# Softmax sums in an attention, SoLU and softplus kernel: reciprocals transposed as four columns and repeated by DMAs, and a planner that reckons loads at 240 GB/s

## The chip, the cores and the metric

The kernel runs on one core of one Trainium2 chip. The metric is device time in microseconds (us). A core has TensorE (PE, with its weight loads shown as PEld), VectorE (DVE), ScalarE (ACT), GpSimd (POOL) and SyncE (SP); each runs its own instructions in order and waits on semaphores for the others. Here SP issues nearly all DMAs.

## The reference

Three stages, all in float32, 2304 rows of 512 between them:

```python
scores = scale * np.matmul(q, k.transpose(0, 1, 3, 2))      # 4 batches, 8 heads, 576 rows, 64 wide
thresh = np.max(scores, axis=-1, keepdims=True) - tau
scores = np.where(scores >= thresh, scores, -1000000000.0)
scores = scores - np.max(scores, axis=-1, keepdims=True)
attn = np.exp(scores)
attn = attn / (np.sum(attn, axis=-1, keepdims=True) + 1e-09)
x = np.matmul(attn, v)                                       # -> x of 2304 x 512
h = x @ w_in                                                 # 512 -> 1024
e = np.exp(h - np.max(h, axis=-1, keepdims=True))
solu = h * (e / (np.sum(e, axis=-1, keepdims=True) + 1e-09))
ln = (solu - mu) / np.sqrt(var + 1e-06) * g_ln               # over the row
x = ln @ w_out                                               # 1024 -> 512
h = x @ w2_in                                                # 512 -> 2048
out = (np.maximum(h, 0) + np.log1p(np.exp(-np.abs(h)))) @ w2_out
```

## The kernel before

**Attention.** Two heads of a batch are a pair, with buffers q, k and v of which four pairs fit. An item is one pair with one or two tiles of 128 query rows (36 items: 8 of one tile, 28 of two); 8 more items take the last 64 rows of four heads. Of a tile, PE makes the scores (L393), DVE their row maximum (L349), ACT the exponential (L350), DVE the threshold and the row sum (L352). PE transposes the weights E (L368), ACT copies them out of PSUM (L371), and PE multiplies them with v (L429), which gives the item's x transposed: 64 rows of one head above 64 of the other, a query to a column. The rows are not divided before that, so each column must be multiplied by the reciprocal of its query's sum.

**The reciprocals, item(), L377 to L434.** The sums of an item are a [128, 2 or 4] tile, a query to a partition. DVE adds 1e-9 and takes the reciprocal (inverse(), L355 to L358). To turn them into rows, ACT spreads each column to 64 columns (rb, L402), PE transposes rb, one full 128x128 transpose for each tile (L408, 64 in all), and ACT copies the result to x in SBUF (L410, two buffers). DVE then multiplies the product in PSUM with x (ml, L432). Until that is done, the product's bank is held; there are four such banks (`w`) for transposes, products, the two later stages' partial sums and fillers.

**The later stages.** The weights of the first two-layer network (w_in, w_out) are loaded as 64-bit words, put together and split into a high and a low part by ACT and DVE (convert(); for four of them PE does the subtraction, L512 and L513). m1_unit() then runs nine units of 256 rows: matmuls (L567), SoLU and normalization, transposes (L610), matmuls (L627, L628), and a store of the result to DRAM (x2s). The second network reads it back (x2m) and runs 16 chunks of its inner width for five blocks of rows (L678, softplus on ACT and DVE, L701). Its output weights (raw_out) have room only once the first network is done.

**The order.** Nothing of the order is written by hand. plan_of() makes a list of operations, each with its engine, two costs in ns (how long it holds the engine, and when its result is there), what it follows, which buffers it takes and uses, and a due time. Plan.order() (L107) then lays them out like a simulation: at each step it takes, of the operations that could start, the one due first; on PE a change of the kind of matmul (R scores, Q scores of the last rows, C product with v, T transposes, G full-width products) adds a price from a table, weighed by STICK (L169). AHEAD says how much later than the earliest one an operation may start and still be chosen. Loads follow one another in one file: 0.5 us after the issue a load moves its bytes at 350 GB/s, and 1.9 us later it has landed (L192, L193). The model also follows PE's clock, and fills early idle time of PE with idle products (filler, L288). The kernel then issues every instruction in the order of the start times found. Due times are the tile's number plus a number from lists (JT, JA, JIT for items; LO and LAGS for units; LD, PREP, PLOAD, W2IN, W2OUT for loads).

Of the kernel before, what the change touches and what calls it, by code (L numbers as in the profile page):

```python
# [9 lines left out]
F32 = mybir.dt.float32  # L10
# [12 lines left out]
P = 128  # L23
# [4 lines left out]
JT = [0.34, 7.73, 0.9, -3.39, 0.54, 0.49, 0.42, 9.02, 0.11, 3.15, -3.13, -0.51, -5.45, 1.01, 1.21, 6.91, -4.6, 8.15, -0.49, -0.88, -1.72, -3.81, 4.75, 9.79, 2.6, 9.72, 9.11, -5.74, -0.21, 2.17, 6.22, 2.62, -2.76, -1.92, 0.89, -0.0, -0.65, 0.66, -0.91, -2.44, -7.92, -1.24, -0.04, -1.57]  # L28
JA = [5.05, -2.61, -3.21, 7.47, 3.78, 3.3, 5.1, 12.84, -4.94, 8.51, 17.33, -7.99, 2.58, -3.17, 5.64, -2.85, 16.01, 16.98, -1.89, 6.77, -1.19, 4.83, 12.32, 18.27, -6.3, 0.39, 12.91, 14.21, 3.05, -5.54, -0.8, -1.5, 4.55, -1.49, -10.83, 10.72, -1.44, -1.37, -9.39, -0.79, 3.84, 3.5, 3.33, 5.39]
LO = [-20.52, -32.27, -28.3, -62.18, -3.33, 1.52, -98.95, 31.75, -24.96]  # L30
# [9 lines left out]
LD = [-11.06, 0.35, 9.2, 14.07, 7.04, 12.77, 7.9, 34.61, 19.66, 38.52, 7.77, 68.68, 10.48, 84.79, 20.67, 17.31, 4.65, 8.82, 1.55, -62.61, -15.71, -19.93, 81.02, 16.74, 91.83, 70.72, 19.84, -5.66, -48.3, 4.79, -22.69, -44.85]  # L40
JIT = [-11.99, -8.79, -5.19, -5.48, 1.8, -10.03, 0.87, -8.03, 6.15, -0.57, 3.09, -24.47, 0.08, 2.59, -34.82, 4.62, 7.64, 16.92, 9.09, 3.38, -14.37, -6.4, -10.15, 3.76, -6.77, -11.43, -14.53, -18.35, -5.02, -26.2, -15.19, -13.01, -2.79, 0.51, -17.2, 8.63, -5.03, -12.19, -11.44, -4.71, -8.08, -1.06, -14.31, -9.49]
# [38 lines left out]
WARM = 130e3  # L80

# [7 lines left out]
class Plan:  # L89
# [17 lines left out]
    def order(self):  # L107
# [12 lines left out]
        mode, dma, done = "", 0, []  # L120
        win, work, slow = 0, {}, False
# [31 lines left out]
        while any(cand.values()):  # L153
# [62 lines left out]
def tile_attention_solu_softplus(ctx: ExitStack, tc: tile.TileContext, q, k, v, tau, w_in, w_out, g_ln, w2_in, w2_out, out):  # L216
# [22 lines left out]
    done = plan_of(nc, ctx, sb, const, ident, minus, pools, stacks, w1t, x2s, q, k, v, tau, w_in, w_out, g_ln, w2_in, w2_out, out).order()  # L239
# [24 lines left out]
def plan_of(nc, ctx, sb, const, ident, minus, pools, stacks, w1t, x2s, q, k, v, tau, w_in, w_out, g_ln, w2_in, w2_out, out):  # L264
# [5 lines left out]
    plan = Plan(dict(w=W_, s=S_, h2=4, E=NE, T=2, eT=NET, x=2, xr=NXR, xrT=1, q=NPAIR, k=NPAIR, v=NPAIR, ln=3, u=2,  # L270
# [22 lines left out]
    def load(eng, out, in_, kb, after=(), takes=(), uses=(), due=0.0):  # L293
        e = sp if eng == "SP" else act
        return op(eng, 620, None, lambda: e.dma_start(out=out(), in_=in_()), after=after, takes=takes, uses=uses, due=due, kb=kb)
# [3 lines left out]
    o_minus = op("ACT", 200, 300, lambda: act.activation(out=minus, in_=ident, func=AF.Copy, scale=-1.0), after=[o_ident], due=-60)  # L299
    o_table = op("ACT", 1300, 1300, lambda: act.preload_act_table_set("natural_log_exp_and_others"), due=-49.5)  # L300

    def queue(what, i):
        return "ACT" if f"{what}{i}" in ON_ACT else "SP"

    def load_qk(p, due):
# [4 lines left out]
        z["kq"], ql = [], []  # L310
# [3 lines left out]
        for h in range(2):  # L314
            r = slice(64 * h, 64 * h + 64)
            ql.append(load(queue("q", p), lambda r=r: q_.t[r, :], lambda h=h: q[p][:, 640 * h:640 * h + 576], 144, takes=() if h else [q_], uses=[q_] if h else (), due=due))
        z["scaled"] = op("ACT", 574, 678, lambda: act.activation(out=q_.t, in_=q_.t, func=AF.Copy, scale=0.125), after=ql, uses=[q_], due=due + 0.5)
# [37 lines left out]
    def inverse(n, w, sums, masks, due):  # L355
        rv = buf("at", "rinv", f"rinv{n}", [P, 4], bufs=4)
        o1 = op("DVE", 80, 170, lambda: dve.tensor_scalar_add(rv.t[:, 0:w], sums.t[:, 0:w], 1e-9), after=masks, takes=[rv], uses=[sums], due=due)
        return rv, op("DVE", 95, 180, lambda: dve.reciprocal(rv.t[:, 0:w], rv.t[:, 0:w]), after=[o1], uses=[rv], due=due)  # L358
# [18 lines left out]
    def item(n):  # L377
# [4 lines left out]
        sums = buf("at", "sums", f"sums{n}", [P, 4], bufs=4)  # L382
        E = [buf("at", "E", f"E{n}_{i}", [P, 1152], bufs=NE) for i in range(nt)]
        masks = {}
        for kk, i in enumerate(ts):
# [8 lines left out]
            sc = op("PE", 970, 1128, emit_s, after=z["kq"] + [z["scaled"]], takes=s, uses=[z["q"], z["k"]], due=j + JIT[n], mode="R")  # L394
# [6 lines left out]
        rb = buf("at", "rb", f"rb{n}", [P, 4, 64])  # L401
# [459 lines left out]
```

## Time and profile before

| | |
|---|---|
| median of 3 runs | 911.25 us (910.9 to 912.68) |
| the profiled execution | 914.37 us, of which its span is 912.6 us |
| PE busy | 899.6 us |
| DVE busy | 690.4 us |
| ACT busy | 591.1 us |
| moved by DMA | 64.63 MB |

The span runs from the first to the last instruction; the time is measured around it. A busy share counts the time in which an instruction is on an engine. Matmuls are pipelined, so a matmul's duration is longer than the distance to the next one's start; the cost of one in a run is read from the starts. A group of lines names what is written, an arrow, and what is read.

### The profile page before, as it was taken

To read this page: it belongs to the slowest core of one execution; us is meant where nothing else is said; L and a number is where in the kernel's file an instruction comes from. 1 tells how busy PE (TensorE), PEld (TensorE's weight loads), DVE (VectorE), ACT (ScalarE), POOL (GpSimd) and SP (SyncE) were. 2 spreads that over 40 slices of the span, in tenths; PEclk is the share of its full clock that TensorE was granted. 3 is DMA by queue.
4 is the path that set the end of the run, shared out by engine and by line. 5 is a ranking of instruction groups with operands and counts; after the bars stand their busy time and mean duration, and the time that the engine had idled before them with its cause. 6 is when DMAs were issued, how large, how long until landed. Compare 5 with 4: busy or idle time off the path is not lost.

```text
span 912.6 us, 14433 instructions
## 1 busy us (share of the span) xinstructions
PE 899.6 (99%) x5458; PEld 709.6 (78%) x5458; DVE 690.4 (76%) x1474; ACT 591.1 (65%) x1159; POOL 0.7 (0%) x6
## 2 busy tenths in 40 slices
PE   8999999999999999999999999999999999999998
PEld 6576676677677677788888878888888888888897
DVE  5999898898777778599958969985556555655565
ACT  6978887997778687676757746764444444444454
POOL 0000000000000000000000000000000000000000
PEclk9999999999999999999999999999999999999999
DMA  9405110230231000164414223430021001100010
GB/s 281 161 1 175 54 30 1 84 83 24 66 109 62 2 1 12 59 219 162 139 59 162 93 98 110 135 119 24 1 92 47 1 1 47 47 0 1 1 47 24
DMA packets 32052, 64.63 MB, mean 71 GB/s; under 512 B 3440, under 2 KB 12912, under 8 KB 31984
## 3 DMA queue, kind: packets, MB, share of 16 engines
q1 hardware_dynamic: 31104, 61.62, 20.8%
q10 hardware_dynamic: 880, 2.10, 0.8%
q8 instruction: 43, 0.70, 0.3%
q14 instruction: 25, 0.20, 0.1%
HBM read 49.55 MB, written 14.16 MB: 70 GB/s over the span
## 4 chain that ended last, share of the span: by engine, by line
PE 83%; DVE 7%; ACT 4%; DMA 4%; issue 1%; SPq 1%; ACTq 0%; DVEq 0%
PE w L701 21%; PE h L678 20%; PE w L567 8%; PE w L368 7%; PE w L429 6%; PE s L393 6%; PE w L627 6%; PE w L628 3%; PE w L610 1%; PE w L472 1%; DMA raw<-in_w_in_dram 1%; DVE E L352 1%; DVE nm L349 1%; PE s L450 1%; DMA q<-in_q_dram 1%
## 5 line engine op out<-in xcount | busy, mean ns | idle before, releaser
L678 PE MATMUL h<-x2m,w2h 128*128 128x512 f32 (+1 forms) x640 | 181.6, 368 | 0.0
L678 PEld LDWEIGHTS h<-x2m,w2h 128*128 128x128 f32 x640 | 116.5, 188 | 21.0
L349 DVE TENSOR_REDUCE nm<-s 128x1 f32<-128x576 f32 x144 | 102.7, 752 | 21.7 <-PE s L393 19.1
L678 PE MATMUL h<-x2m,w2l 128*128 128x512 f32 (+1 forms) x320 | 117.7, 368 | 0.0
L701 PE MATMUL w<-wo2h,gh 128*128 128x512 f32 x288 | 112.9, 392 | 1.1 <-ACT wo2h L503 1.1
L701 PE MATMUL w<-wo2l,gh 128*128 128x512 f32 x288 | 113.0, 393 | 0.6 <-DVE wo2l L505 0.6
L352 DVE SCALAR_TENSOR_TENSOR E<-E,etau 128x576 f32<-128x576 f32 x128 | 101.1, 815 | 16.3 <-ACT E L350 14.9
L701 PE MATMUL w<-wo2h,gl 128*128 128x512 f32 x288 | 112.7, 391 | 0.0
L371 ACT COPY eT<-w 128x512 f32<-128x512 f32 (+1 forms) x188 | 92.9, 554 | 19.5 <-PE w L368 18.9
L689 ACT ACTIVATE t<-h 128x512 f32<-128x512 f32 (+1 forms) x80 | 44.3, 554 | 90.9 <-PE h L678 90.9
L627 PE MATMUL w<-lhl,wo1h 128*128 128x512 f32 x288 | 102.8, 397 | 0.0
L350 ACT ACTIVATE E<-s,nm 128x576 f32<-128x576 f32 x128 | 91.6, 756 | 11.2 <-DVE nm L349 11.0
L691 DVE TENSOR_SCALAR gw<-t 128x512 f32<-128x512 f32 (+1 forms) x80 | 31.8, 399 | 80.3 <-ACT t L690 80.1
L693 ACT ACTIVATE gw<-gw 128x512 f32<-128x512 f32 (+1 forms) x80 | 47.1, 589 | 61.1 <-DVE t L692 60.0
L393 PE MATMUL s<-k,q 64*128 64x288 f32 x512 | 83.9, 429 | 2.0 <-ACT E L350 1.4
L628 PE MATMUL w<-lhl,wo1l 128*128 128x256 f32 x288 | 80.7, 280 | 0.0
L429 PE MATMUL w<-eT,v 128*64 128x256 f32 (+1 forms) x720 | 77.8, 364 | 1.6 <-ACT eT L371 1.5
L368 PE MATMUL w<-ident,E 128*128 128x128 f32 x576 | 78.4, 279 | 0.0
L368 PEld LDWEIGHTS w<-ident,E 128*128 128x128 f32 x576 | 63.6, 141 | 17.4 <-issue 6.4
L694 DVE SCALAR_TENSOR_TENSOR gw<-h,gw 128x512 f32<-128x512 f32 (+1 forms) x80 | 51.0, 637 | 33.1 <-ACT gw L693 32.0
L429 PEld LDWEIGHTS w<-eT,v 128*64 128x64 f32 x720 | 47.1, 138 | 28.0 <-ACT eT L371 4.4
L678 PEld LDWEIGHTS h<-x2m,w2l 128*128 128x128 f32 x320 | 60.3, 188 | 10.1
(107 smaller groups left out, 1573.2 us busy)
## 6 DMA issues: line engine op xcount, KB each, us to landing
x2s<-x SPq DMA_DIRECT2D x36, 256.0 KB, 2.0
x2m<-x2s SPq DMA_DIRECT2D x18, 512.0 KB, 6.0
raw_in<-in_w_in_dram SPq DMA_DIRECT2D x16, 512.0 KB, 3.8
raw_out<-in_w_out_dram SPq DMA_DIRECT2D x16, 512.0 KB, 3.6
v<-in_v_dram SPq DMA_DIRECT2D x15, 320.0 KB, 3.4
q<-in_q_dram SPq DMA_DIRECT2D x28, 144.0 KB, 3.6
out_dram<-yo SPq DMA_DIRECT2D x15, 256.0 KB, 2.1
raw<-in_w_out_dram SPq DMA_DIRECT2D x3, 1024.0 KB, 7.8
```

The lines of the kernel that those rows point to most:

```text
L349: mx = op("DVE", 668, 750, lambda: dve.tensor_reduce(out=nm.t, in_=src(), axis=AX.XY, op=ALU.max, negate=True), after=[after], takes=[nm], ...
L350: ex = op("ACT", 638, 741, lambda: act.activation(out=dst().rearrange("p (a b) -> p a b", a=2), in_=src(), func=AF.Exp, bias=nm.t, scale=1.0),
L352: return op("DVE", 739, 900, lambda: dve.scalar_tensor_tensor(out=dst(), in0=dst(), scalar=etau, in1=dst(), op0=ALU.is_ge, op1=ALU.mult, a ...
L368: pe.transpose(bk.t[:, P * i:P * i + P], b_.t[:, c:c + P], ident)
L371: copies.append(op("ACT", occ, occ + 111, lambda: act.copy(out=eT.t[:, 0:width], in_=bk.t[:, 0:width]), after=[g], uses=[bk, eT], due=due))
L393: pe.matmul(s[h].t[:, nh, 0:288], z["q"].t[r, c:c + P], z["k"].t[r, 288 * nh:288 * nh + 288], start=True, stop=True)
L429: pe.matmul(o_.t[64 * h:64 * h + 64, 0:W], z["v"].t[:, vcols(c, h)], e[8 if c == 8 else 4 * h + c](), start=(i == 0), stop=(i == 4))
L567: pe.matmul(ps.t, x__[:, part, :], w_[:, part, 512 * n:512 * n + 512], start=(part == 0 and j_ == 0), stop=(part == 3 and j_ == 2))
L627: pe.matmul(o.t.rearrange("p (a q) -> p a q", a=2), w1t["wo1h"][:, c, P * m:P * m + P], lhl.t[:, :, c, :], start=(c == 0), stop=False)
L628: pe.matmul(o.t[:, 0:256], w1t["wo1l"][:, c, P * m:P * m + P], lhl.t[:, 0, c, :], start=False, stop=(c == 7))
L678: pe.matmul(ps.t[:, 0:n], w2t["in", a, c][:, part, :], x.t[:, b_, part, 0:n], start=(part == 0 and j_ == 0), stop=(part == 3 and j_ == 2))
L701: pe.matmul(ys[j].t, g_.t[:, P * j:P * j + P], w2t["out", a, c], start=(c == 0 and i == 0), stop=(c == NC2 - 1 and i == 2))
```

## The change

Four things. The reciprocals, a [128, w] tile with w of 2 or 4, are transposed as they are: one transpose an item gives [w, 128] in PSUM, ACT copies it to r4 (two buffers), SP writes it to a DRAM tile rs and reads it back with two DMAs, one for each head, which repeat each row to 64 partitions of x. q of the first pair is loaded and scaled in two pieces, columns 0 to 191 and 192 to 575, and the scores of its first tile wait for the first piece alone. The planner reckons loads at 240 GB/s rather than 350, the first not before 2.5 us, adds 1.8 us to the landing of the two reads, starts with PE's clock low, and has other costs for some operations. All lists of due times, STICK and AHEAD have other values.

```diff
-JT = [0.34, 7.73, 0.9, ...]
+JT = [1.36, -8.49, 3.75, ...]
...
-LAGS = [246.6, 85.18, 40.19, 34.26, 25.47, 27.39, 40.09, 53.12, 104.33]
-D_MAX, D_MASK, D_SUM, D_T, D_X, D_AV = 1.74, 10.86, 3.2, 3.73, 1.71, -15.06
-D_MT, D_POST, D_OUT = 8.93, 2.73, -15.88
-AHEAD = dict(PE=0, DVE=0, ACT=0, SP=20, POOL=20, X=20)
+LAGS = [303.47, 28.54, 2.25, 23.85, 74.05, 70.66, 42.32, 71.52, 102.15]
+D_MAX, D_MASK, D_SUM, D_T, D_X, D_AV = -7.0, 24.35, 5.23, 2.69, -23.16, 4.18
+D_MT, D_POST, D_OUT = 12.15, -13.18, -25.57
+AHEAD = dict(PE=20, DVE=100, ACT=20, SP=200, POOL=20, X=20)
...
-YLAG = 4.72
-PLOAD = -16.03
-W2IN = 60.61
-W2OUT = -5.81
+YLAG = 6.0
+PLOAD = -125.2
+W2IN = -10.08
+W2OUT = -10.85
 TURNED = 4
-STICK = 0.48
-PREP = [-18.8, -45.68, -12.55, 12.05, 71.4, 119.39, -150.07, 43.1]
+STICK = 1.85
+PREP = [-67.7, -87.23, -5.21, 2.75, 195.54, 111.21, -68.22, 79.77]
...
+FIRST = 2500
...
-        mode, dma, done = "", 0, []
-        win, work, slow = 0, {}, False
+        mode, dma, done = "", FIRST, []
+        win, work, slow = 0, {}, True
...
-                dma = max(dma, s + 500) + o.kb * 1024 / 350
-                o.end = dma + 1900
+                dma = max(dma, s + 500) + o.kb * 1024 / 240
+                o.end = dma + 1900 + (o.fin or 0)
...
+    rs = [dram.tile([4, P], F32, tag=f"rs{n}", name=f"rs{n}") for n in range(len(items_of()))]
...
-        z["scaled"] = op("ACT", 574, 678, lambda: act.activation(out=q_.t, in_=q_.t, func=AF.Copy, scale=0.125), after=ql, uses=[q_], due=due + 0.5)
+        cuts = [0, 192, S] if p == 0 else [0, S]
+        z["scaled"] = []
+        for a, e in zip(cuts, cuts[1:]):
+            ql = []
...
+            z["scaled"].append(op("ACT", occ, occ + 104, lambda a=a, e=e: act.activation(out=q_.t[:, a:e], in_=q_.t[:, a:e], func=AF.Copy, scale=0.125), after=ql, uses=[q_], due=due + 0.5))
...
-        rb = buf("at", "rb", f"rb{n}", [P, 4, 64])
-        o3 = op("ACT", 187 if nt == 1 else 310, 298 if nt == 1 else 410, lambda: act.copy(out=rb.t[:, 0:w, :], in_=rv.t[:, 0:w].unsqueeze(2).to_broadcast([P, w, 64])), after=[o2], takes=[rb], uses=[rv], due=jl + D_SUM)
         rbk = bank()
+        r4 = buf("at", "r4", f"r4{n}", [4, P], bufs=2)
         x = buf("at", "x", f"x{n}", [P, 256], bufs=2)
-
-        def emit_r():
-            for i in range(nt):
-                pe.transpose(rbk.t[:, P * i:P * i + P], rb.t[:, 2 * i:2 * i + 2, :].rearrange("p a b -> p (a b)"), ident)
-        rg = op("PE", 109 * nt, 109 * nt + 163, emit_r, after=[o3, o_ident], takes=[rbk, x], uses=[rb], due=jl + D_X, mode="T")
-        xc = op("ACT", 162 if nt == 1 else 263, 270 if nt == 1 else 395, lambda: act.copy(out=x.t[:, 0:W], in_=rbk.t[:, 0:W]), after=[rg], uses=[rbk, x], due=jl + D_X)
+        rg = op("PE", 64, 227, lambda: pe.transpose(rbk.t[0:w, 0:P], rv.t[:, 0:w], ident), after=[o2, o_ident], takes=[rbk], uses=[rv], due=jl + D_X, mode="T")
+        rc = op("ACT", 160, 265, lambda: act.copy(out=r4.t[0:w, :], in_=rbk.t[0:w, 0:P]), after=[rg], takes=[r4], uses=[rbk], due=jl + D_X)
+        wr = load("SP", lambda: rs[n][0:w], lambda: r4.t[0:w, :], 1, after=[rc], uses=[r4], due=jl + D_SUM)
+        xc = [load("SP", lambda h=h: x.t[64 * h:64 * h + 64, 0:W].rearrange("p (i q) -> p i q", q=P), lambda h=h: bass.AP(tensor=rs[n].tensor, offset=rs[n].offset + P * h, ap=[[0, 64], [2 * P, nt], [1, P]]), 16 * nt, late=1800, after=[wr], takes=[x] if h == 0 else (), uses=[x] if h else (), due=jl + D_SUM) for h in range(2)]
...
-        ml = op("DVE", ... after=[av, xc], uses=[o_, x, xt], due=jl + D_AV + JA[n])
+        ml = op("DVE", ... after=[av] + xc, uses=[o_, x, xt], due=jl + D_AV + JA[n])
```

The buffers of sums and reciprocals go from four to eight. The costs of ten operations of convert(), of the scaling in tail_item() and of two steps of m1_unit() are other numbers; the operations are the same.

## Rows read from the trace of the kernel before

**Rows 1.** The page's head and its engine shares, whole span.
```profile
span 912.6 us, 14433 instructions
PE 899.6 (99%) x5458; PEld 709.6 (78%) x5458; DVE 690.4 (76%) x1474; ACT 591.1 (65%) x1159; POOL 0.7 (0%) x6
```

**Rows 2.** Stretches: length; busy PE, PEld, DVE, ACT, POOL; PEclk; DMA share, GB/s.
```profile
25.00:50.00 25.00, 23.97 (x146) 15.43 (x144) 24.00 (x58) 23.63 (x48) 0.00 (x0) 0.93 0.30 111
50.00:75.00 25.00, 25.00 (x208) 17.68 (x208) 24.70 (x53) 18.62 (x38) 0.00 (x0) 1.00 0.13 40
...
525.00:550.00 25.00, 23.27 (x98) 18.63 (x98) 17.19 (x33) 12.45 (x23) 0.00 (x0) 0.93 0.31 106
...
600.00:625.00 25.00, 25.00 (x112) 20.71 (x111) 19.82 (x35) 14.88 (x26) 0.00 (x0) 1.00 0.12 44
```

**Rows 3.** The page's chain of waits, shares of the span by engine.
```profile
PE 83%; DVE 7%; ACT 4%; DMA 4%; issue 1%; SPq 1%; ACTq 0%; DVEq 0%
```

**Rows 4.** Groups by line and form: count | busy us, mean ns | idle before.
```profile
L368 PE MATMUL w<-ident,E 128*128 128x128 f32 x576 | 78.4, 279 | 0.0
...
L408 PE MATMUL w<-ident,rb 128*128 128x128 f32 x64 | 14.1, 292 | 0.5 <-ACT rb L402 0.5
...
L402 ACT COPY rb<-rinv 128x256 f32<-128x256 f32 x28 | 11.7, 416 | 10.6 <-DVE rinv L358 9.7 <-DVE m_t L596 0.8
...
L429 PE MATMUL w<-eT,v 128*64 128x128 f32 x160 | 11.2, 293 | 1.5 <-ACT eT L371 1.5
...
L410 ACT COPY x<-w 128x256 f32<-128x256 f32 x28 | 10.9, 390 | 6.2 <-PE w L408 6.1
```

**Rows 5.** Timeline of the start, ACT and then PE: start us, length us.
```profile
6.01 0.68 ACT L317 ACTIVATE q<-q 128x576 f32<-128x576 f32 x1 [0.84 <-DMA q<-in_q_dram]
...
6.74 1.31 PE L393 MATMUL s<-k,q 64*128 64x288 f32 x8 [0.47 <-ACT q L317]
...
15.71 1.31 PE L429 MATMUL w<-eT,v 128*64 128x128 f32 x20
...
17.12 1.04 PE L368 MATMUL w<-ident,E 128*128 128x128 f32 x8
```

**Rows 6.** Timeline of PE, about 100 us and the last transposes.
```profile
99.02 2.38 PE L429 MATMUL w<-eT,v 128*64 128x256 f32 x20
101.33 0.44 PE L408 MATMUL w<-ident,rb 128*128 128x128 f32 x2
101.70 1.24 PE L393 MATMUL s<-k,q 64*128 64x288 f32 x8
...
508.55 1.91 PE L610 MATMUL w<-ident,h 128*128 128x128 f32 x16
```

**Rows 7.** Timeline of PE at the hole, then a piece of the chain.
```profile
541.17 0.39 PE L678 MATMUL h<-x2m,w2l 128*128 128x512 f32 x1
542.69 0.50 PE L701 MATMUL w<-wo2h,gh 128*128 128x512 f32 x1 [1.14 <-ACT wo2h L503]
543.79 0.72 PE L701 MATMUL w<-wo2l,gh 128*128 128x512 f32 x1 [0.59 <-DVE wo2l L505]
544.30 0.63 PE L701 MATMUL w<-wo2h,gl 128*128 128x512 f32 x1
...
533.64 5.85 DMA raw_out<-in_w_out_dram
```

**Rows 8.** DMA issues: count, KB each, median us from issue to landing.
```profile
x2s<-x SPq DMA_DIRECT2D x36, 256.0 KB, 2.0
...
raw<-in_w_in_dram SPq DMA_DIRECT2D x4, 512.0 KB, 10.8
...
tau_sb<-in_tau_dram SPq DMA_DIRECT2D x1, 0.5 KB, 4.1
```

**Rows 9.** Timeline of DVE: reciprocal of an item, then its product.
```profile
36.48 0.15 DVE L358 RECIPROCAL rinv<-rinv 128x2 f32<-128x2 f32 x1
...
40.83 0.29 DVE L432 TENSOR_TENSOR xr<-w,x 128x128 f32<-128x128 f32 x1
```

More of the change, by code (lines that the diff above doesn't have):

```diff
@@ L393, in emit_s @@
                     pe.matmul(s[h].t[:, nh, 0:288], z["q"].t[r, c:c + P], z["k"].t[r, 288 * nh:288 * nh + 288], start=True, stop=True)
-            sc = op("PE", 970, 1128, emit_s, after=z["kq"] + [z["scaled"]], takes=s, uses=[z["q"], z["k"]], due=j + JIT[n], mode="R")
+            sc = op("PE", 970, 1128, emit_s, after=z["kq"] + z["scaled"][0:1 if i == 0 else 2], takes=s, uses=[z["q"], z["k"]], due=j + JIT[n], mode="R")
             scores.append(sc)
@@ L431, in item @@
         av = op("PE", a_occ, a_occ + 170, emit_av, after=copies + [z["vl"]], takes=[o_] + tk1, uses=eTs + [z["v"]] + us1, due=jl + D_AV + JA[n], mode="C")
-        ml = op("DVE", 200 if nt == 1 else 336, 284 if nt == 1 else 420, lambda: dve.tensor_tensor(out=xt.t[:, h_, c0:c0 + W], in0=o_.t[:, 0:W], in1=x.t[:, 0:W], op=ALU.mult), after=[av, xc], uses=[o_, x, xt], due=jl + D_AV + JA[n])
+        ml = op("DVE", 200 if nt == 1 else 336, 284 if nt == 1 else 420, lambda: dve.tensor_tensor(out=xt.t[:, h_, c0:c0 + W], in0=o_.t[:, 0:W], in1=x.t[:, 0:W], op=ALU.mult), after=[av] + xc, uses=[o_, x, xt], due=jl + D_AV + JA[n])
         for t in ts:
@@ L450, in emit_s @@
                         pe.matmul(s[i].t[o:o + 64, nh, 0:288], zs[i]["q"].t[r, c:c + 64], zs[i]["k"].t[r, kc:kc + 288], start=True, stop=True)
-        sc = op("PE", 970, 1128, emit_s, after=[a for z in zs for a in z["kq"] + [z["scaled"]]], takes=s, uses=[z[a] for z in zs for a in "qk"], due=j + JIT[n], mode="Q")
+        sc = op("PE", 970, 1128, emit_s, after=[a for z in zs for a in z["kq"] + z["scaled"]], takes=s, uses=[z[a] for z in zs for a in "qk"], due=j + JIT[n], mode="Q")
         scores.append(sc)
-        sums = buf("at", "sums", f"sums{n}", [P, 4], bufs=4)
+        sums = buf("at", "sums", f"sums{n}", [P, 4], bufs=8)
         T = [buf("at", "T", f"T{n}_{i}", [P, 640], bufs=2) for i in range(2)]
@@ L487, in convert @@
         w_ = lambda: lw().bitcast(F32)
[L488 removed]
+        a1 = op("ACT", 69 + 1022 * k_, 181 + 1008 * k_, lambda: act.activation(out=hw().bitcast(F32), in_=hw().bitcast(F32), func=AF.Copy, scale=2.0 ** -112), after=after, uses=[raw], due=due - 0.1)
         a2 = op("DVE", 70 + 535 * k_, 150 + 540 * k_, lambda: dve.tensor_scalar(out=lw(), in0=lw(), scalar1=29, scalar2=None, op0=ALU.logical_shift_right), after=after, uses=[raw], due=due)
@@ L499, in convert @@
             for i in range(2):
-                h = op("ACT", 525, 620, lambda i=i: act.activation(out=hi()[:, i, :], in_=w_()[:, i, :], func=AF.Copy, scale=scale(i)), after=[a4, o_g], uses=[raw], due=due)
-                low.append(op("DVE", 602, 692, lambda i=i: dve.scalar_tensor_tensor(out=lo()[:, i, :], in0=w_()[:, i, :], scalar=scale(i), in1=f(hi()[:, i, :]), op0=ALU.mult, op1=ALU.subtract), after=[h], uses=[raw], due=due))
+                h = op("ACT", 666, 794, lambda i=i: act.activation(out=hi()[:, i, :], in_=w_()[:, i, :], func=AF.Copy, scale=scale(i)), after=[a4, o_g], uses=[raw], due=due)
+                low.append(op("DVE", 665, 752, lambda i=i: dve.scalar_tensor_tensor(out=lo()[:, i, :], in0=w_()[:, i, :], scalar=scale(i), in1=f(hi()[:, i, :]), op0=ALU.mult, op1=ALU.subtract), after=[h], uses=[raw], due=due))
             return low
-        a5 = op("ACT", 100 + 850 * k_, 200 + 850 * k_, lambda: act.copy(out=hi(), in_=w_()), after=[last], uses=[raw], due=due)
+        a5 = op("ACT", 68 + 1004 * k_, 158 + 1018 * k_, lambda: act.copy(out=hi(), in_=w_()), after=[last], uses=[raw], due=due)
         if not turned:
```

47 lines of the change are left out of this document (24 added, 23 removed).

## The prediction

> **What bounds the kernel now.** I read the page's engine shares first: TensorE is busy for 899.6 of 912.6 us, the next engine, VectorE, for three quarters [rows 1]. The table of stretches then says where this holds. From 25 us to the end PE is close to 25.0 of every 25 us; in the last 400 us nothing else comes near it, while from 25 to 75 us DVE is at 24.0 and 24.7 of 25 beside it, so that early on two engines share the bound [rows 2]. The chain of waits agrees: 83% of the span is PE, 7% DVE, 4% DMA [rows 3]. PE time is therefore the currency. What PE does is of three kinds: matmuls at their steady spacing; changes from one kind of matmul to another (scores, transposes, attention times v, full-width products), which the timeline shows as gaps between starts; and true waits. Counted through the PE timeline, some 225 changes cost time: the first leads to the scores at 6.74 us [rows 5], the last to the transposes at 508.55 us [rows 6].
>
> The true waits are few: the start (the first scores begin at 6.74 us, behind the scaled q [rows 5]), some low clock before 50 us (granted 0.93 of full in 25 to 50 us, so about 25 x 0.07 = 1.75 us of work lost [rows 2]), and one hole at 541 us.
>
> **The profiled execution.** Its span is 912.6 us, its own time 914.37, so 1.8 us lie around the span; the median of the runs is 911.25, that is 3.1 below the profiled one. I add changes to 914.37 and take 3.1 off at the end.
>
> **Part 1, the transposes.** Removed: 64 full 128x128 transposes (L408) [rows 4]. Their spacing: the run of 8 that starts at 17.12 lasts 1.04 us, of which 0.28 is one's own duration [rows 4], so (1.04 - 0.28) / 7 = 0.109 us each [rows 5]. 64 x 0.109 = 7.0 us of PE. Added: 36 transposes, one an item, with 2 or 4 weight columns and 128 moving columns. No row shows such a one. The nearest below: a matmul that also moves 128 columns, on 64 weight columns, comes every (1.31 - 0.29) / 19 = 0.054 us (run of 20 at 15.71 [rows 5], duration of one [rows 4]); above: the old transpose, 0.109. I take 0.06, near the lower row, because it is the narrow weight load that the two have in common: 36 x 0.06 = 2.2. Gain 4.9 us, between 5.1 (at 0.054) and 3.1 (at 0.109).
>
> The Trainium skill (TensorE: Matmul & The Clock Gate, LDWEIGHTS) states that a weight load costs by its columns, columns / 1.2 in ns, whatever the rows. By that 128 columns are 107 ns, which is what the old spacing would be if the load were not hidden, and 4 columns are nothing; the sum by it is the lower end. No run here shows a load of 4 columns.
>
> **Part 2, ScalarE.** The spread copy (L402) goes: 416 ns x 28 and the smaller ones of 8 items, some 14 us; the copy of x (L410, 390 ns x 28) becomes a copy of 128 columns [rows 4]. ACT is relieved by about 17 us before 380 us. ACT bounds nothing there (rows 2: 18.6 to 23.6 of 25), so I count this as nothing; it shortens the softmax chain when PE waits for it, and what covers it is PE's backlog. If the cover were thin, it would be a small gain, not a loss.
>
> **Part 3, the three DMAs of an item.** 36 writes of 1 or 2 KB to DRAM and 72 reads that repeat a row to 64 partitions: 108 issues more on SP, in order. SP waits at each read until the write has landed, and behind it on SP stand the loads of later q, k, v, the weight loads and the x2 stores (whose two buffers hold PE's banks). Who waits for the reads is the product L432, and while it waits it holds one of 4 banks that PE needs. Price: an undisturbed store lands in 2.0 us; a 0.5 KB load within the opening burst takes 4.1, and 512 KB behind other weights 10.8 [rows 8]. Write, second issue and read are thus 2 x 2.0 and some issue time, about 5 us at the least, to which the small copy and transpose come: about 6.5 from reciprocal to x. In the trace the product comes 4.2 us after the reciprocal at the tightest (36.63 to 40.83 [rows 9]), and under 7 us for ten of the 36 items, six of these before 71 us; later ones have 8 to 30 us. The schedule is laid out anew with these latencies in it (1.9 + 1.8 us per read), so I expect most to be hidden by moving products later. I take +0.8 us; the ends are 0 and about +10, the shortfalls of those ten items (6.5 less their lags, added up: 9 us) all on PE.
>
> **Part 4, the start.** q of the first pair is scaled in two pieces, of which the first, 192 of 576 columns, needs a third of the load and of the 0.68 us of scaling [rows 5]. Scaling falls to about 0.3; the smaller load saves up to 1 us more, as k has to land as well. But then DVE's softmax is next, so I take -0.7 of 0 to -1.4.
>
> **Part 5, the schedule.** All due times, orders and lags are drawn anew, with loads at 240 instead of 350 GB/s. Two things can be priced. First, the hole at 541 us: PE idles 1.14 + 0.59 us, then its matmuls take 0.63 instead of 0.39 us because the clock has fallen; the chain shows the load of raw_out, 5.85 us [rows 7]. With the clock at 0.93 in 525 to 550 us [rows 2] that is 1.73 + 1.75 = 3.5 us. The old planner takes 0.5 + 512 KB / 350 + 1.9 = 3.9 us for such a load, the new one 4.6, still short of 5.85, but nearer; I take -1.5 of 0 to -3.5. Second, the changes of kind. A lone pair between attention-times-v and scores takes 101.70 - 101.33 = 0.37 us for 2 x 0.11 of work, so 0.15 for such a change [rows 6]; 225 of them are some 34 us. STICK, the planner's price on them, goes from 0.48 to 1.85, but the due times that compete with it are spread four times as wide. I take -1.0, of +4 to -4 (a tenth of the changes more or fewer, 3.4 us, rounded up).
>
> **The sum.** -4.9 - 0.7 - 1.5 + 0.8 - 1.0 = -7.3: 914.4 - 7.3 = 907.1 profiled, 904.0 as a median.
>
> **Rivals.**
>
> A, slower: the small DMAs arrive late. Place: before 75 us, where weights are loaded and lags are tightest. If an rs write or an x read stands behind a burst of weight loads, it lands not after 2.0 but after up to 10.8 us [rows 8], 8.8 late; SP holds everything behind it, the product holds its bank, PE stops, and after the stop the clock is low (1.75 us as at 541). One such stop on PE is 10.5 us; with half of it covered by other items, 5, and three of them 15. Time: -7.3 - 0.8 + 15 = +6.9, 918. It decides from 7 us of PE waiting on. For it: ten tight items. Against: the planner keeps one file of DMAs and moves weight loads later (PLOAD -16 to -125).
>
> B, no change: the thin transposes are a kind of their own on PE. A change costs 0.15 or more; of the 36 old groups seven stand between other transposes and 19 beside one on one side, where today they cost no change. 7 x 0.35 (two changes more) + 19 x 0.2 (one more) = 6 us back: 904 + 6 = 910. The gain of part 1 would be eaten. For it: matmuls with 64 output columns are listed as 128*64 in the trace, so narrower ones may be listed narrower, too [rows 4]. Against: nothing, as no row shows it. The Trainium skill (TensorEngine Tiling (Array Packing), Key Properties) says that changing the tiling mode drains the engine; the gap of row 101.33 agrees in kind, and by that rule B holds if the narrow output picks a narrow tile.
>
> C, much faster: the new order finds what the old one left. Hole gone (-3.5), start at its best (-1.4), changes a tenth down (-3.4), transposes -4.9, DMAs 0: -13.2, 898.
>
> **How the numbers follow.** Forecast 904 (between 900 and 909) 0.50; C 0.17; B 0.15; A 0.18. A measurement of this kernel tells about 0.2% from no change, 1.8 us: faster is under 909.4, slower over 913.1. Faster: the forecast, C, and a small part of B, 0.70; same: the rest of B and the edge of A, 0.13; slower 0.17. The range leaves out the far end of C (0.07) and most of A (0.13): 897 to 914.
>
> **What would show it.** Part 1: 36 transposes with w columns, 0.05 to 0.07 us to the next start; 0.2 or more there is B. Part 3: the product L432 waiting for DMA x, and PE idle behind it, before 75 us, is A. Part 4: first scores before 6.2 us. Part 5: no idle and full clock around the first L701; fewer than 225 changes. I am wrong if PE's busy share falls below 97%, or if the last 400 us change by more than the hole.

## The result, and the profile after

The changed kernel took 926.42 us (median of 4 runs, 925.71 to 927.58) where the kernel before took 911.39 beside it: ratio 1.0145, 95% interval 1.0115 to 1.0176. It is slower by about 15 us, where 904.0 had been forecast and 914 was the upper end of the range. The profiled execution has a span of 925.8 us, 13.2 more than that of before.

The page of after: head, busy shares, and the chain of waits by engine.

```profile
span 925.8 us, 14575 instructions
PE 901.6 (97%) x5432; PEld 706.5 (76%) x5432; DVE 697.7 (75%) x1474; ACT 579.2 (63%) x1123; POOL 0.7 (0%) x6
...
PE 91%; DVE 4%; ACT 3%; issue 1%; DMA 1%; ACTq 0%; POOLq 0%; SPq 0%; POOL 0%; DVEq 0%
```

Against [rows 1] and [rows 3]: PE is busy two points less of a longer span, and the chain doesn't point at DMA at all; its DMA share fell from 4% to 1%. None of its 36 products waits for a read (four wait for PE, 7.6 us in all), so there is no queue of products standing at the new transfers. The stretches of after (columns as in [rows 2]) say where the time went:

```profile
25.00:50.00 25.00, 19.89 (x81) 9.71 (x81) 23.11 (x50) 18.93 (x34) 0.00 (x0) 0.86 0.36 132
50.00:75.00 25.00, 23.30 (x231) 17.27 (x231) 24.38 (x54) 22.08 (x45) 0.00 (x0) 1.00 0.10 34
75.00:100.00 25.00, 20.06 (x158) 13.59 (x155) 17.38 (x34) 15.74 (x29) 0.00 (x0) 0.93 0.57 166
...
550.00:575.00 25.00, 22.14 (x90) 17.59 (x89) 22.29 (x41) 15.37 (x27) 0.00 (x0) 0.93 0.33 115
```

In [rows 2] PE was at 23.97 and 25.00 in the first two stretches. I counted every matmul at its steady spacing (fillers left out, a thin transpose at 0.105 us) and summed in stretches of 25 us: at 100 us after has 13.0 us less of work done than before; by 350 us 7.5 of that is won back, because work of the first linear layer (L572) was drawn forward; by 450 us 7.6 is lost again; the hole in the second layer makes 3.0 more, 16.1 in all. After has 3.2 us less to do, so 12.9 of the 13.2 are placed. The last 325 us are alike.

Three places carry it. First, products come late. The first two views are one line of the trace each, first and last start after "median/max": the product of after (L437), then that of before (L432); the third is from the timeline of after, PE's first attention-times-v.

```profile
L437 DVE TENSOR_TENSOR xr<-w,x x36: 259/418/426, 41.0 to 433.0; 128x256 f32<-128x256 f32 x28, 128x128 f32<-128x128 f32 x8
```

```profile
L432 DVE TENSOR_TENSOR xr<-w,x x36: 276/421/428, 17.2 to 386.6; 128x256 f32<-128x256 f32 x28, 128x128 f32<-128x128 f32 x8
```

```profile
12.73 1.31 PE L434 MATMUL w<-eT,v 128*64 128x128 f32 x20 [0.76 <-ACT eT L379]
```

What PE wrote from 12.73 on is multiplied at 41.0 us, where before it was multiplied at 17.2. The next two results of this kind, written from 23.40 and 28.10 us on, are multiplied at 44.1 and 47.2. So from 29 to 41 us three of the four banks stand full, and what else PE writes has to go through the one that is left, where PE stands until ACT has copied it out (timeline of PE):

```profile
23.40 1.31 PE L434 MATMUL w<-eT,v 128*64 128x128 f32 x20
...
28.10 1.31 PE L434 MATMUL w<-eT,v 128*64 128x128 f32 x20
...
32.43 1.17 PE L517 MATMUL w<-raw,ident 128*128 128x512 f32 x2 [2.43 <-ACT eT L379]
...
34.89 2.07 PE L517 MATMUL w<-raw,ident 128*128 128x512 f32 x2 [1.06 <-ACT w1l L520]
```

Not all of this is the round trip. In the trace the packets of the first two items' reads (512 bytes each) move between 27.9 and 32.0 us, so their x is there 9 and 12 us before the products at 41.0 and 44.1. The planner keeps its loads in one file: by its own reckoning the first read lands at 39.3 us, behind 4 MB of weight loads (17.5 us at 240 GB/s), and the product follows that. No product of after comes sooner than 8.5 us behind its reciprocal (median of 36: 11.1); before the tightest was 4.2, the median 9.4, and 13 were under 8. The last product has moved from 386.6 to 433.0 us.

Second, one stop of ScalarE. From the timeline of after, ACT and then PE:

```profile
84.47 0.86 ACT L379 COPY eT<-w 128x512 f32<-128x512 f32 x2 [6.48 <-DMA k<-in_k_dram]
...
85.38 4.07 PE L434 MATMUL w<-eT,v 128*64 128x256 f32 x20 [4.94 <-ACT eT L379]
```

And from its chain of waits (start, length, what):

```profile
76.17 7.71 DMA k<-in_k_dram
```

ACT, which issues some loads itself, stood 6.48 us at the issue of a load of q, by the profile until a load of k was in. PE stood 4.94 us behind it, and its next 20 matmuls took 4.07 us against 2.38 for 20 such at 99 us in [rows 6]: TensorE went on, for a while, at the lower of its two levels (1.2 GHz; granted 0.93 over this stretch).

Third, the hole that the new order was to close has moved from 541 to 555 us and grown ([rows 7]; idle 2.13 + 0.73 us now, 1.14 + 0.59 before):

```profile
555.59 0.50 PE L706 MATMUL w<-wo2h,gh 128*128 128x512 f32 x1 [2.13 <-ACT wo2h L508]
556.82 0.80 PE L706 MATMUL w<-wo2l,gh 128*128 128x512 f32 x1 [0.73 <-DVE wo2l L510]
```

### The profile page after: what moved, and what is told of

It reads as the page before. It is cut to its first block, busy times and chain, and to the rows that moved or that the text cites. A ratio compares the mean times of both kernels' runs of the same rounds, so it can differ in the third digit from the quotient of the medians.

```text
span 925.8 us, 14575 instructions
## 1 busy us (share of the span) xinstructions
PE 901.6 (97%) x5432; PEld 706.5 (76%) x5432; DVE 697.7 (75%) x1474; ACT 579.2 (63%) x1123; POOL 0.7 (0%) x6
## 4 chain that ended last, share of the span: by engine, by line
PE 91%; DVE 4%; ACT 3%; issue 1%; DMA 1%; ACTq 0%; POOLq 0%; SPq 0%; POOL 0%; DVEq 0%
PE w L706 21%; PE h L683 21%; PE w L572 10%; PE s L401 8%; PE w L376 7%; PE w L632 7%; PE w L434 7%; PE w L633 4%; PE w L615 2%; PE w L477 1%; PE s L455 1%; PE w L517 1%; DMA k<-in_k_dram 1%; DVE E L360 1%; PE w L290 1%
## 5 line engine op out<-in xcount | busy, mean ns | idle before, releaser
L701 ACT CAST gh<-gw 128x512 fp32r<-128x512 f32 (+1 forms) x80 | 46.4, 580 | 117.2 <-PE w L706 115.2
L702 DVE TENSOR_TENSOR gl<-gw,gh 128x512 fp32r<-128x512 f32 (+1 forms) x80 | 51.0, 637 | 68.4 <-ACT gh L701 68.4
L632 PEld LDWEIGHTS w<-lhl,wo1h 128*128 128x128 f32 x288 | 54.1, 188 | 15.2 <-issue 2.7
```

What stands on the lines that cost most here:

```text
L632: pe.matmul(o.t.rearrange("p (a q) -> p a q", a=2), w1t["wo1h"][:, c, P * m:P * m + P], lhl.t[:, :, c, :], start=(c == 0), stop=False)
```

## The experiments

Two theories stood against each other at first: the loss is in the new order (Theory 1), or in the round trip of the reciprocals, wherever it is put (Theory 2).

**The new path in the old order.** Every old instruction keeps its place; the spread copy becomes nothing, the transpose and copy of x become the thin ones, and the three transfers are issued on SP where x was copied.

```diff
-            for i in range(nt):
-                pe.transpose(rbk.t[:, P * i:P * i + P], rb.t[:, 2 * i:2 * i + 2, :]..., ident)
+            pe.transpose(rbk.t[0:w, 0:P], rv.t[:, 0:w], ident)
...
+            act.copy(out=rb.t[0:w, :], in_=rbk.t[0:w, 0:P])
+            sp.dma_start(out=rs[n][0:w], in_=rb.t[0:w, :])
+            for h in range(2):
+                sp.dma_start(out=x.t[64 * h:64 * h + 64, 0:W]..., in_=...)
```

> The order of the kernel before is kept, instruction for instruction; only the reciprocals go the new way (36 thin transposes, a copy of [w, 128], a write and two reads on SP, issued where the copy of x stood). Theory 1, the loss of 15 us sits in the new order: here the thin transposes save 64 x 0.109 less 36 x 0.105 = 3.2 us, and the early products wait for reads that stand behind the six weight loads issued at 13.0 to 17.1 us; product 0 stood at 17.2 us and those loads land up to 28.5 us, so 5 to 12 us are lost at the start: 913 to 921 us. Theory 2, the loss sits in the operations and their DMAs, whatever the order: 922 us or more. Theory 3, the small DMAs are hidden anyway: 908 us.

Measured: 958.14 us, ratio 1.0497 (1.0459 to 1.0534). The path costs 46 us in the old order, as Theory 2 had it (922 us or more), though no theory had named so much. Its waits (us in all, times, longest):

```profile
DVE xr L438 <- DMA x<-rs: 35.8, 13, 5.5
ACT q L318 <- DMA q<-in_q_dram: 15.7, 9, 2.9
```

One of its stretches:

```profile
50.00:75.00 25.00, 18.98 (x110) 12.58 (x112) 17.19 (x45) 13.96 (x28) 0.00 (x0) 0.73 0.03 9
```

And an item's way on its timeline, reciprocal, transpose, copy, write, reads and product:

```profile
60.30 0.16 DVE L359 RECIPROCAL rinv<-rinv 128x2 f32<-128x2 f32 x1
...
64.16 0.37 PE L408 MATMUL w<-ident,rinv 128*2 128x128 f32 x1
...
64.56 0.26 ACT L411 COPY r<-w 2x128 f32<-2x128 f32 x1 [1.06 <-PE w L408]
64.85 0.23 SPq L412 DMA_DIRECT2D rs<-r  x1
65.99 1.09 SPq L414 DMA_DIRECT2D x<-rs  x2
69.10 0.29 DVE L438 TENSOR_TENSOR xr<-w,x 128x128 f32<-128x128 f32 x1 [3.42 <-DMA x<-rs]
```

Undisturbed, with the DMA engines at 3% of their time, the way from the end of the small copy (64.82) to the product (69.10) is 4.3 us, and from the start of the transpose, which came 3.7 us behind the reciprocal in PE's order, 4.9. 13 products waited for a read, and a stop of PE is paid twice, since the granted clock fell to 0.73 in this stretch. That is rival A as it was written, and the planner's new order avoids it: in after no product waits for a read.

**The same, on a queue of its own.** The three transfers are issued by GpSimd, so that nothing stands behind them.

```diff
-            sp.dma_start(out=rs[n][0:w], in_=rb.t[0:w, :])
+            pool.dma_start(out=rs[n][0:w], in_=rb.t[0:w, :])
```

> As the kernel with the old order and the new reciprocals, but the write and the two reads are issued by the idle GpSimd, on its own queue, so they stand behind no load on SP and SP waits for none of them. Theory 1 (the loss sits in the new order): the transposes' 3.2 us are seen, the early products still wait a little for data that shares the DMA engines with the weight loads: 907 to 911 us. Theory 2 (the operations and their DMAs cost it in any order): 918 us or more.

Measured: 967.86 us, 1.0612 (1.057 to 1.0655). The products' wait grew and that for q fell:

```profile
DVE xr L438 <- DMA x<-rs: 56.4, 12, 9.2
...
ACT q L318 <- DMA q<-in_q_dram: 8.7, 6, 2.3
```

This too is Theory 2's (918 us or more): the tight items pay for the round trip itself, whichever queue it takes.

**The new order without its transfers.** After's order; writes and reads are left out, and the product multiplies by ones.

```diff
+        for o in (wr, *xc):
+            o.fn = lambda: None
...
-in1=x.t[:, 0:W], op=ALU.mult), after=[av] + xc
+in1=one[0][:, 0:W], op=ALU.mult), after=[av] + xc
```

> The order of the changed kernel is kept; the write of the sums and the two reads are left out, and the products are multiplied with ones instead of the reciprocals (so the division by the sums is left out). Theory 1 (the loss sits in the new order, in which the products are put so late that they wait for no read): 922 to 926 us, as the changed kernel, and the product of the first item still starts at about 41 us. Theory 2 (the small DMAs cost it, on SP, on the semaphores or on the DMA engines): 915 us or less.

Measured: 925.07 us, 1.0129 (1.0073 to 1.0184), which can't be told from after. Its first weak stretch is the same to the hundredth (19.89 us busy, clock 0.86 in after):

```profile
25.00:50.00 25.00, 19.89 (x82) 10.03 (x83) 23.25 (x52) 19.12 (x34) 0.00 (x0) 0.86 0.31 118
```

So in the new order no cost of running the transfers shows, and Theory 1 holds there: what costs is the order that was laid around them.

**The new order, ACT's later loads on SP.** One line; the loads that ACT issues while it computes go to SP.

```diff
-        e = sp if eng == "SP" else act
+        e = sp if eng == "SP" or due > -40 else act
```

> The order of the changed kernel is kept; the loads of q, v and weights that ACT issues after the start are issued by SP at the same place of the order. In the changed kernel ACT stands still from 78 to 84.5 us at the issue of a q load, until a k load has landed, and PE idles 4.94 us behind it, with the clock low after it (0.93 of full in 75 to 100 us). Theory 1 (that stall is one piece of the loss, and it is worth its idle time and its clock): 919 to 922 us. Rival (the q load itself was late, and SP gets it no sooner): 925 to 927 us.

Measured: 920.04 us, 1.0081 (1.0054 to 1.0108). ACT's stop at 78 to 84 us is gone, and that stretch is full:

```profile
25.00:50.00 25.00, 21.11 (x90) 10.57 (x90) 23.25 (x52) 19.49 (x34) 0.00 (x0) 0.86 0.38 141
50.00:75.00 25.00, 23.30 (x234) 17.09 (x233) 24.74 (x53) 21.52 (x45) 0.00 (x0) 1.00 0.07 21
75.00:100.00 25.00, 25.00 (x208) 17.16 (x205) 23.73 (x48) 20.13 (x36) 0.00 (x0) 1.00 0.56 169
```

926.4 - 920.0 = 6.4 us hang on these issues, most of it on that one stop (PE's busy time of 75 to 100 us rose by 4.94); some 8 stay.

**The thin transposes alone.** The old order with the first experiment's edit, less the transfers; the product multiplies by ones.

> The order of the kernel before, every instruction in its old place, with the thin transposes and the small copy of Parts 1 and 2 alone: the spread copy (ScalarE) and the 64 full transposes are out, 36 thin ones and a copy of 4 x 128 are in. There is no write and no read, and the product multiplies by a tile of ones, so the division by the sums is left out. Theory T1 (a thin transpose takes TensorE as long as a full one, 0.105 us, and every microsecond taken off PE is a microsecond of the time): 64 x 0.109 - 36 x 0.105 = 3.2 us less than before, ratio 0.9965. Theory T2 (the forecast's 0.06): 4.9 us less, 0.9946. Theory T3 (PE stands on something else often enough that less work on it gains nothing): within 1 us of before. Theory T4 (ScalarE's relief of some 17 us counts early on, where two engines share the bound): more than 6 us less.

Measured: 908.18 us, 0.9932 (0.9911 to 0.9953): 6.2 us less, between 4.3 and 8.1. The forecast's 4.9 lies within; the 3.2 by the spacing doesn't. The spacing on the timeline of this kernel is nevertheless that of a full transpose:

```profile
12.50 0.66 PE L375 MATMUL w<-ident,E 128*128 128x128 f32 x4
12.99 0.27 PE L414 MATMUL w<-ident,rinv 128*2 128x128 f32 x1
13.10 0.71 PE L375 MATMUL w<-ident,E 128*128 128x128 f32 x5
```

The thin one (12.99) holds PE 0.11 us, like its neighbours, and neither change of width costs a gap. Most of what lies between 3.2 and 6.2 is the clock: of the 21 executions of the kernel before that belong to this run 13 had a granted clock below 1.000 (0.993 to 0.998), of this kernel's ten only three. The executions at 1.000 have a median of 912.1 us before (8 of them) and 908.2 here (7), 3.9 us less. Why the clock fell less often isn't shown. The hole of [rows 7] takes part in it and varies from one execution to the next: PE's idle time at this place is 0.24 us in this profiled execution, and 0.39 in one of the next kernel, whose order there is the old one, too.

**The start alone.** The kernel before with q of the first pair loaded and scaled in two pieces.

```diff
-lambda h=h: q[p][:, 640 * h:640 * h + 576], 144, ...
+lambda h=h: q[p][:, 640 * h:640 * h + (192 if p == 0 else 576)], 144, ...
-        z["scaled"] = op("ACT", 574, 678, lambda: act.activation(out=q_.t, ...
+        z["scaled"] = op("ACT", 574, 678, lambda: [act.activation(out=q_.t[:, a:e], ...) for a, e in (((0, 192), (192, S)) ...
```

> The kernel before in its old order with Part 4 alone: q of the first pair is loaded and scaled in two pieces. T1: first scores some 0.8 us earlier (5.9 instead of 6.7 us) and the time 0.8 us less, ratio 0.9991. T2: the gain at the first scores is given back, because the softmax and the later q and k loads set the pace of the first 20 us: within 0.3 us of before.

Measured: 914.8 us, 1.0013 (0.9993 to 1.0032): no gain, and the expected 0.9991 is outside. From its timeline, ACT's scaling of q, then PE's fillers and first scores:

```profile
4.88 0.78 ACT L326 ACTIVATE q<-q 128x192 f32<-128x192 f32 x2
...
1.35 5.31 PE L288 MATMUL w<-ident 128*128 128x128 f32 x28 [1.35 <-POOL ident masks.py:199]
...
6.60 1.24 PE L402 MATMUL s<-k,q 64*128 64x288 f32 x8
```

q is scaled from 4.88 us on, not from 6.01 [rows 5], but the scores stand behind the 28 fillers of the old order until 6.6 us (after has 20 of them). So this run doesn't test what an earlier q is worth. The start also varies by itself: the same old start gave first scores at 6.74 [rows 5] and, in the kernel with the thin transposes, at 7.50, more apart than the 0.8 that was to be won.

**The planner's new rates alone.** The kernel before with its operations and its numbers; what changes is the planner's rate of loads, the time of its first load and the clock it starts with.

```diff
-        mode, dma, done = "", 0, []
-        win, work, slow = 0, {}, False
+        mode, dma, done = "", 2500, []
+        win, work, slow = 0, {}, True
...
-                dma = max(dma, s + 500) + o.kb * 1024 / 350
+                dma = max(dma, s + 500) + o.kb * 1024 / 240
```

> The kernel before with its own operations, due times and lags, of which only the planner's model is changed as in the change: loads at 240 instead of 350 GB/s, no load before 2.5 us, a low clock at the start. The old numbers were drawn for the old model, so the order that comes out is not a tuned one. T1 (the slower loads put the order of the first 100 us out of step, as in the changed kernel, and the rest follows): 10 to 30 us slower, with the loss before 100 us. T2 (the order is robust, and the loss of the changed kernel comes from its new lists and from the DMA path in the plan): within 5 us of before. In both, if the hole at 541 us hangs on the planner's rate of the weight loads, it is gone here.

Measured: 928.96 us, 1.0164 (1.0127 to 1.0201). The old numbers don't suit the new rates, and where there was one hole PE now has longer stops, the longest within the second network:

```profile
516.41 1.22 PE L678 MATMUL h<-x2m,w2h 128*128 128x512 f32 x2 [5.40 <-DVE m_t L592]
```

With these numbers the slower rate doesn't close the hole, as Part 5 had it, but makes others. As the numbers were drawn for other rates, this says nothing of how good the rates are with numbers of their own.

**The new path with the old rates.** All three transfers are operations of the planner, at its old rates, with the old numbers as a start and a search over them on the planner's own model.

```diff
-        o3 = op("ACT", 187 if nt == 1 else 310, ...
+        wr = load("SP", lambda: rs[n][0:w], lambda: r4.t[0:w, :], 1, after=[rc], ...
+        xc = [load("SP", lambda h=h: x.t[64 * h:64 * h + 64, 0:W]..., late=1800, after=[wr], ...) for h in range(2)]
```

> All 36 items take the new way, as operations that the planner knows (writes and reads with their latencies), but the planner keeps its old rates (350 GB/s, full clock at the start), and due times and lags start from the old ones and are moved by a search. Theory T1 (the loss of the changed kernel is that its order has to wait out the round trip in all 36 items, whatever the rates): again slower than before, by 3 to 10 us, with the loss before 100 us. Theory T2 (the loss comes from the new rates and the list drawn for them): as before or faster, -3 to +2 us.

Measured: 922.93 us, 1.0125 (1.0093 to 1.0158). With rates and numbers of another origin the loss is nearly that of after, and again no product waits for a read, none comes sooner than 8.1 us behind its reciprocal (median 12.1), and about half of the loss (5.2 of 10.0 us by the count of work) stands in the same stretches:

```profile
25.00:50.00 25.00, 21.69 (x118) 12.30 (x119) 23.56 (x53) 21.01 (x38) 0.00 (x0) 0.93 0.33 123
...
75.00:100.00 25.00, 22.91 (x187) 16.19 (x188) 23.01 (x44) 20.20 (x39) 0.00 (x0) 1.00 0.39 115
```

So the new rates aren't needed for a loss: the two orders that wait out the round trip in all 36 items lost 11 and 15 us. The planner's own reckoning says as much: laid out with each kernel's numbers, its list ends at 903.2 us before, at 910.4 here, and at 916.9 (by its slower rates) in after. What isn't shown is that no better numbers exist: no order of the old path was drawn anew beside these, so a search that ended badly can't be told from the round trip.

**Only the late items.** Where the product comes late anyway, the new path should be a gain. The first try named items by the list, which counts the tails too; it took 16 items, four of them tight. The edit of the first experiment stands under the first branch, the old code under the second:

```diff
+DMA_ITEMS = (12, 13, 16, 17, 19, 20, 21, 22, 24, 25, 26, ..., 34, 35)
...
+        if n in DMA_ITEMS:
...
+        else:
...
```

> The kernel before in its old order, where only 20 of the 36 items (12, 13, 16, 17, 19 to 22 and 24 to 35) take the new way of the reciprocals: thin transpose, small copy, write, two reads. These are items whose product didn't wait for its reads when all 36 took the new way in the old order; the other 16 keep the spread copy and the two full transposes. Theory T1 (the round trip costs only where the product follows sooner than it takes; later it is free, and the saved PE time counts): 40 x 0.109 - 20 x 0.105 = 2.3 us less than before, or 20/36 of the 6.2 us that the thin transposes gave alone, 3.4 less: ratio 0.996 to 0.9975. Theory T2 (108 more transfers on SP's queue cost in themselves, by holding later loads back behind waits): as a part of the 46 us lost with all 36, 5 us slower or more. Theory T3 (the saved PE time counts only where PE alone bounds): within 1 us of before.

Measured: 934.14 us, 1.0235 (1.021 to 1.026). One of the tight items shows what a single late read costs; timeline, SP's transfers, then DVE and PE:

```profile
101.41 0.47 SPq L416 DMA_DIRECT2D rs<-rb  x1
103.67 1.29 SPq L418 DMA_DIRECT2D x<-rs  x2
...
107.07 0.42 DVE L453 TENSOR_TENSOR xr<-w,x 128x256 f32<-128x256 f32 x1 [5.48 <-DMA x<-rs]
...
108.20 0.79 PE L588 MATMUL w<-w1h,xh 128*128 128x512 f32 x1 [3.79 <-ACT xh L578]
```

DVE, in order, stands 5.48 us, PE 3.79, and in 108.20 a 512-column matmul takes 0.79 instead of 0.39 us [rows 7], at the lower level. Its variant, with nearly all due times and lags moved by a search on a model that doesn't know these transfers, was worse still:

> The same 20 items the new way, and due times and lags moved a little by a search on the planner's own model with the old rates (it doesn't know the transfers of these items). If the model is good to a microsecond the order gains about 1 us over the old one: 3 to 4.5 us less than before, ratio 0.995 to 0.997. If small moves in the order bring the tight items back to waiting, or if the model isn't that good, 0 to 10 us slower than the frozen order.

Measured: 947.4 us, 1.0381 (1.0343 to 1.0418). The products' wait for reads rose from 11.5 us (4 times) to 17.4 (5), so items are back at waiting, as the second half of its expectation said; the loss is more than it allowed.

Then 19 items by their place in time, all with 7.8 us or more from reciprocal to product:

```diff
-DMA_ITEMS = (12, 13, 16, 17, 19, 20, 21, 22, 24, 25, 26, ..., 34, 35)
+DMA_ITEMS = (15, 18, 19, 22, 24, 25, 26, 28, 29, 31, 32, 34, 35, 37, 38, 40, 41, 42, 43)
```

> The list of items also numbers the tails, so the run with 20 named items in truth gave the new way to 16 items, the 12th, 15th, 16th and 18th to 30th in time; four of them (12th, 15th, 16th, 19th) have 5.3 to 7.7 us from reciprocal to product in the kernel before. This run names them by their place in time: 19 items, the 14th, 17th, 18th, 20th to 23rd and 25th to 36th, with at least 7.8 us from reciprocal to product and 5.9 us from the copy of x to the product in the kernel before, take the new way in the old order, their transfers on SP's queue. Theory T1 (the round trip costs only where the product follows sooner than it takes): 38 x 0.109 - 19 x 0.105 = 2.1 us less than before, or 19/36 of 6.2, 3.3: ratio 0.9964 to 0.9977. Theory T2 (SP, which stands at each read until the write has landed, sends the loads of later q and k later, and ScalarE stands at their scaling): 5 us slower or more, and ScalarE's wait for q well over the 7.0 us of before.

Measured: 924.75 us, 1.0146 (1.0124 to 1.0168). No product waits for a read, and yet 13 us are lost. The wait for q, which was 7.0 us in 7 times before:

```profile
ACT q L321 <- DMA q<-in_q_dram: 19.8, 12, 2.7
```

Three views of one place: SP's transfers, ACT's scaling of q, and the stretch (busy PE, granted clock, DMA share, GB/s):

```profile
158.32 0.43 SPq L416 DMA_DIRECT2D rs<-rb  x1
160.58 1.23 SPq L418 DMA_DIRECT2D x<-rs  x2
...
162.50 1.24 SPq L299 DMA_DIRECT2D q<-in_q_dram  x2
```

```profile
166.34 0.68 ACT L321 ACTIVATE q<-q 128x576 f32<-128x576 f32 x1 [1.14 <-DMA q<-in_q_dram]
```

```profile
150.00:200.00 50.00, 45.08 (x343) 0.93 0.24 71
```

**The late items on GpSimd's queue.** The same 19 items, with the issues of the second experiment.

> The same 19 items, their writes and reads issued by GpSimd on its own queue, so that no load stands behind them. T1: as the run before, 2.1 to 3.3 us less than before, both alike. T2: the loss of the run before is gone here, 2.1 to 3.3 us less than before (if GpSimd's round trip, some 5 to 7 us from copy to use, still fits in the 5.9 us), and ScalarE's wait for q is at 7 us or less. Theory T3 (both slower by 5 us or more): the small transfers cost in another way than by these waits.

Measured: 911.95 us, 1.0004 (0.9984 to 1.0023). The loss is gone, by the queue alone. ACT's wait for q, SP's issue of the same load, and the stretch:

```profile
ACT q L321 <- DMA q<-in_q_dram: 8.2, 7, 1.7
```

```profile
159.99 1.18 SPq L299 DMA_DIRECT2D q<-in_q_dram  x2
```

```profile
150.00:200.00 50.00, 49.38 (x420) 1.00 0.28 81
```

T2's cause holds. With the transfers on its queue SP stands at a write until ACT's small copy is made (111.3 us in 17 waits over the run) and at the reads until the write has landed (20.1 us in 19), so the loads of q behind them are issued late, the one shown by 2.5 us (162.50 against 159.99); ScalarE stands at their scaling, PE behind it. T2's figures don't hold: the wait for q is 8.2 us where 7 or less was named, and the gain of 2 to 3 us that the saved PE time should have left isn't seen. The interval, from 0.9984 on, leaves out the expected 0.9964 to 0.9977, the executions with a granted clock of 1.000 have the same median as those of the kernel before (911.1 us), and where the gain went isn't known. No version ran faster than before with the division in it.

So the path has two prices in an order that doesn't know it: the products' wait (12 or 13 items) and SP's queue (13 us for 19 items).

## Why the prediction was wrong, point by point

**What bounds the kernel.** Right: PE time is the currency, and PE's busy share below 97% had been named as a sign of error; with 97% it stands just at it. By the count most of the loss stands at 100 us.

**Part 1 (-4.9).** The term lies within what was measured, by luck; its working failed. The thin transposes alone gave -6.2 (-8.1 to -4.3), but a thin one holds PE 0.10 to 0.11 us and not 0.06 (12.99 to 13.10 above; 24.65 to 24.75 in after). By the spacing the term is 64 x 0.109 - 36 x 0.105 = 3.2, the lower bound that I gave, and the executions at full clock say 3.9. I took the row with the narrow weight load as the nearest; the rows that count were those of transposes. The Trainium skill (TensorE: Matmul & The Clock Gate, LDWEIGHTS) prices a weight load by its columns; for 2 or 4 columns an estimate by that is next to nothing, and the trace shows the spacing of 128 columns all the same, so the weight load didn't set it. No run here shows what did.

**Part 2 (0).** ACT's relief is inside the -6.2 and can't be told apart.

**Part 3 (+0.8, ends 0 and +10).** This is the step that failed. The round trip was sized well enough for a quiet stretch (6.5 us from reciprocal to x; measured 4.9 from the start of the transpose at 64.16 to the product at 69.10, 4.3 of it behind the copy); among the first weight loads it was longer, a write of the first experiment issued at 23.2 us had its reads issued only at 32.9. What failed is the sentence that most of it would be hidden by moving products later, for +0.8 us, and that its worst case is the shortfall of ten items, 9 us. In the old order it is 46 us, because a stop is paid on DVE, on PE and then in the clock, and because SP's queue makes the loads late also where no product is (13 us of it for 19 items). Moved out of the way, it is not free either: an order in which each product is 8 us behind its reciprocal lost 11 us with the old rates and some 8 with the new (920.0, with ACT's stop taken out), with 5.2 of 10.0 and 5.6 of 8.6 us of work missing at 100 us, by the count. There two engines share the bound, and the products that wait hold the banks that PE needs, three of four from 29 to 41 us in after. The first was in [rows 2]; I read it as PE's backlog covering the path. In the second of these orders the missing work is made up by 350 us and lost again by 575, so the count tells where work is missing and not, for all of it, what cost it.

**Part 4 (-0.7).** After's first scores begin at 5.92 us, as named. What that is worth no run shows: in the run made for it the old order's fillers held the scores back, and the start varies by as much as was to be won.

**Part 5 (-2.5, of +4 to -7.5).** Wrong. The hole stayed. The new order also has a stop of ACT that no view of before could show, 6.4 us. The kinds change 301 times where before they changed 277 times (runs of like matmuls in the timeline), more, not fewer; at the 0.15 us of the prediction that is some 3.6 us, an estimate, and the term's sign was wrong.

**Rivals.** A (918) had the right mechanism, the late small transfers, at the right place, before 75 us, but as PE waiting behind the product; in after it appears as an order that gives the wait away beforehand, and no row says "DMA x". With 0.18 it was priced too low: I held the planner's knowledge of the latencies against it, though that only changes the form of the payment. B (910) is refuted: thin ones are listed as 128*2, a kind of their own, and yet stand between full ones without a gap. The Trainium skill (TensorEngine Tiling (Array Packing), Key Properties), by whose rule a change of mode drains the engine, was no reason for B: the rows from 12.50 to 13.10 show no gap at either side of the listed 128*2. C (898) is refuted by the hole and the kinds.

**What stays open.** Why the clock fell less often with the thin transposes alone; where the gain of the late items on GpSimd's queue went; and whether some other order of the new path would be as fast as before. That the order carries the loss is shown by the run without transfers; that the round trip makes every order of this path slower is argued. The two that ran, drawn in different ways, lost 11 and 15 us, which bears on it and doesn't prove it.

## What to carry to other kernels

A latency that a planner knows is not hidden by that: ask how much other work there is at the place where it is put, and read that from the busy shares of all engines in that stretch, not from the mean slack of the items. Where the planner is at hand, ask it for its own total of the new order (916.9 against 903.2 us here). When a small transfer goes on a queue that also carries loads, price every instruction behind its wait (here 13 us for 57 small transfers which no consumer waited for), and try another queue first. Test a removed cost alone in the frozen old order before the order is redrawn: the thin transposes and the new path, so run, showed at once which was worth something. See that nothing of the old order hides what is tested, as the fillers did with q.

## What the hardware showed

- A transpose with 2 or 4 weight columns and 128 moving columns holds PE 0.10 to 0.11 us, the same as one with 128; no gap stood between the two kinds.
- Write to DRAM and read back, repeated to 64 partitions, took 4.3 us from the end of the copy to use with the DMA engines at 3% of their time; issued by GpSimd it wasn't shorter (5.4 us, from 56.53 to 61.97 us of the second experiment; reads land 2.6 us after their issue):

```profile
x<-rs POOLq DMA_DIRECT2D x56, 64.0 KB, 2.6
```

- ScalarE stood 6.48 us at its own load issue in after. Without the small transfers it stood at the same place, and the trace then names another load (timeline of ACT):

```profile
82.63 0.86 ACT L385 COPY eT<-w 128x512 f32<-128x512 f32 x2 [5.26 <-DMA raw<-in_w_out_dram]
```

What the issue waited for can't be told from that; that moving the issue to SP removes the stop is shown.
